# The opening of an FFT mixer with a two-layer network behind it: stage A on four array quarters, bias over 128 rows, turning by products over row halves

## The chip, the core and the metric

One core of a Trainium2 chip runs the kernel. The metric is the device time of one execution in microseconds (us), as the median of several runs. Engines: PE multiplies matrices (its weight loads are shown as PEld), DVE and ACT work on elements, SP issues most transfers, ACT a few; 16 DMA engines carry them.

## What is computed

x has 8 batches of 3008 x 256 numbers, in float32.

```python
X = np.fft.rfft(x, axis=1)
Yr = Xr @ w_r - Xi @ w_i + b_r
Yi = Xr @ w_i + Xi @ w_r + b_i
Yr = sign(Yr) * maximum(abs(Yr) - 0.01, 0)      # the same for Yi
y = np.fft.irfft(Yr + 1j * Yi, n=3008, axis=1)
h = maximum(y.reshape(24064, 256) @ w_in, 0)    # w_in: 256 x 2048
out = h * h @ w_out                             # w_out: 2048 x 256
```

## The kernel before

The transform of length 3008 is split as 47 x 64. Stage A multiplies x by a table over the 47 points; it gives 24 complex rows r, the others being conjugates. Stage B, for a pair of rows, transforms over the 64 points (`psb`), mixes by w_r and w_i (`psm`, with the bias as the first product of the sum), shrinks, and turns back over the 64 points (`psc`). Stage D goes back over the 47 points (`psd`) and leaves y in the chunk `xt`, split into a high and a low part. Between the stages the data go through DRAM: `s` holds the rows of A for B (`eva` stored, `bin` read back) and those of B for D (`evc` stored, `din` read back).

A long loop of rounds then runs the network: round r makes 256 of the 2048 hidden values for one chunk of about 508 tokens (`ph`, `mm1`) and, two rounds later, adds their share of the output (`po`, `mm2`). Stages A, B and D of the following batches are laid between its products. Batch 0 as a whole, stage A of batch 1 and the preparation of both weight matrices have to come earlier: that is the opening, the function `start()`.

`start()` does not issue instructions directly. It hands operations to a `Queue`: an engine (or a choice of two), a cost, a due date, the operations that must be over (`after`), those that must be issued (`behind`), and the buffer pool it takes from. `Queue.run()` simulates the engines with these costs and emits the instructions in the order that comes out; each engine then works through its own instructions strictly in that order. Dates and costs only set the order: on the chip every instruction waits for its data. The dates are lists of constants (`PAIR_DUE`, `A1_DUE`, `W_DUE`, `A2_DUE`); a load can be planned no earlier than its date unless the rings run empty.

Steps of the opening that the change touches, with their lines:

- Stage A of batch 0: x0 in nine loads (L454) over 96 partitions, which hold two points n2 times 47 rows (and two of filling). Sixteen products with the block table tU (96 x 96) over 512 columns each (L460), each copied by DVE (L472) and stored in two halves of 12 rows r: the first half on ACT's queue at once, the second on SP's queue (L476) once the loads of the first two pairs are issued.
- Stage A of batch 1: sixteen loads (L491, dates from `A1_DUE`), sixteen products (L460), copies (L498) into three `ev1` buffers, sixteen stores (L502).
- Twelve pairs: read-back (L524), `psb` (L320), high and low parts `xh`, `xl` (L533, L537), bias (L541: `one` is 33 x 128, `rows` 33 x 512; b's high part stands in row 0, its low part in row 32), eight products with the high part (L545), four with the low part (L550), `t` (ACT, L554), `z` (DVE, L558).
- Turning: two DVE copies (L564) and two ACT steps with a sign (L571) move the halves of z, 64 partitions each, under each other into `zh`; one product with tM (128 x 128) over 512 columns follows (L575), then the copy `evc` (L579).
- Weights: 16 blocks of 512 KB (L673, L675), each with a string of ACT and DVE steps (L684 to L746).
- The end: `din` for the first two groups of tokens (L619, L624), `psd` (L368), `dv` and `dx` (L632, L375), `xt` (L639, L642). Then the pools of the opening are given back and `ph` of round 0 can begin (L286 to L288).

Products of float32 operands show as two PE records each (the two of a 512-column product stand 0.43 us apart); those of the float32r type as one. In the loop, batches 2 to 7 have their stage A as four products of 47 x 64 against 512 columns, on the four quarters of the array (L845).

## Time and profile before

| | |
|---|---|
| median of 3 runs | 2592.77 us (2590.5 to 2596.39) |
| profiled execution | 2591.96 us, of which 2590.2 us from the first to the last instruction (the span) |
| PE, DVE, ACT busy | 99%, 81%, 77% of the span |
| mean granted PE clock | 0.996 |

Busy time of an engine counts only its computing instructions. A span of PE is longer than its step: records of consecutive products overlap, so the distance between two starts is the price of one. The granted clock is given as a share of 2.4 GHz; 0.50 is 1.2 GHz.

### The profile page before, as it was taken

How to read it: one execution, taken by the hardware profiler on the slowest of the kernel's cores; microseconds unless marked ns; L12 is line 12 of the kernel's file. 1: busy time of each engine (PE TensorE's matmuls, PEld its weight loads, DVE VectorE, ACT ScalarE, POOL GpSimd, SP SyncE). 2: the span in 40 equal slices, each digit the busy share in tenths (PEclk: the TensorE clock that was granted, in tenths of full speed). 3: DMA queues.
4: the chain of work that ended last, by engine and by line, in shares of the span. 5: the costliest groups of instructions: out<-in, count | busy, mean ns of one | idle time of the engine just before them, and what ended most of it. 6: DMA issues, size and time to landing. Idle time of an engine off the chain costs nothing.

```text
span 2590.2 us, 42989 instructions
## 1 busy us (share of the span) xinstructions
PE 2556.8 (99%) x16664; PEld 2273.7 (88%) x16664; DVE 2103.9 (81%) x3441; ACT 1990.5 (77%) x3048; POOL 0.2 (0%) x4
## 2 busy tenths in 40 slices
PE   7899999999999999999999999999999999999999
PEld 4589987999889998899988999899998999999998
DVE  6888887888878888788887888778887888877777
ACT  4687886788778787788877878778886788777776
POOL 0000000000000000000000000000000000000000
PEclk9999999999999999999999999999999999999999
DMA  8611114111241112311132111321114111001010
GB/s 251 219 52 41 42 51 142 48 44 50 66 124 32 49 41 84 105 40 41 47 113 79 36 41 50 124 61 36 57 41 129 49 46 56 32 25 35 17 32 17
DMA packets 125361, 171.35 MB, mean 66 GB/s; under 512 B 13157, under 2 KB 88751, under 8 KB 125159
## 3 DMA queue, kind: packets, MB, share of 16 engines
q1 hardware_dynamic: 124139, 166.99, 20.8%
q8 instruction: 133, 2.18, 0.3%
q10 hardware_dynamic: 1020, 1.61, 0.2%
q14 instruction: 69, 0.57, 0.1%
HBM read 93.50 MB, written 74.97 MB: 65 GB/s over the span
## 4 chain that ended last, share of the span: by engine, by line
PE 96%; DMA 2%; DVE 1%; ACT 1%; SPq 0%; issue 0%; ACTq 0%; DVEq 0%
PE ph L286 13%; PE ph L288 13%; PE ph L287 13%; PE po L286 12%; PE po L287 12%; PE po L288 12%; PE psd L368 3%; PE psb L320 3%; PE psm L288 2%; PE psm L287 2%; PE psm L286 2%; PE psa L845 2%; DMA s<-eva 1%; PE psm L545 1%; PE psa L460 1%; PE psc L287 1%
## 5 line engine op out<-in xcount | busy, mean ns | idle before, releaser
L1091 ACT CAST gh<-g 128x762 fp32r<-128x762 f32 (+3 forms) x768 | 682.4, 927 | 325.4 <-PE po L288 284.5
L1100 DVE TENSOR_TENSOR gl<-g,gh 128x762 fp32r<-128x762 f32 (+3 forms) x768 | 805.5, 1070 | 107.3 <-ACT gh L1091 106.4
L286 PE MATMUL po<-gh,wo 128*128 128x254 f32 (+1 forms) x2688 | 765.4, 285 | 0.0
L287 PE MATMUL po<-gl,wo 128*128 128x254 f32 (+1 forms) x2688 | 753.7, 280 | 0.4 <-DVE gl L1100 0.4
L288 PE MATMUL po<-gh,wo 128*128 128x254 f32 (+1 forms) x2688 | 753.0, 280 | 0.0
L286 PE MATMUL ph<-xt,wi 128*128 128x508 f32 (+2 forms) x1536 | 609.9, 397 | 8.9 <-ACT g L1038 5.2
L288 PE MATMUL ph<-xt,wi 128*128 128x508 f32 (+2 forms) x1536 | 598.4, 390 | 0.0
L287 PE MATMUL ph<-xt,wi 128*128 128x508 f32 (+2 forms) x1536 | 597.3, 389 | 0.0
L286 PEld LDWEIGHTS po<-gh,wo 128*128 128x128 f32 x2688 | 510.0, 190 | 35.9 <-issue 29.2
L1038 ACT ACTIVATE g<-ph 128x508 f32<-128x508 f32 (+1 forms) x768 | 410.9, 588 | 157.3 <-PE ph L288 154.5
L287 PEld LDWEIGHTS po<-gl,wo 128*128 128x128 f32 x2688 | 509.8, 190 | 6.8 <-DVE gl L1100 0.6
L288 PEld LDWEIGHTS po<-gh,wo 128*128 128x128 f32 x2688 | 509.8, 190 | 0.0
L1047 DVE TENSOR_TENSOR g<-g 128x508 f32<-128x508 f32 (+1 forms) x384 | 261.3, 680 | 279.3 <-ACT g L1039 272.7
L1039 ACT ACTIVATE g<-g 128x1016 f32<-128x1016 f32 (+1 forms) x384 | 401.3, 1045 | 12.2
L286 PEld LDWEIGHTS ph<-xt,wi 128*128 128x128 f32 x1536 | 290.1, 189 | 65.3 <-issue 9.7
L288 PEld LDWEIGHTS ph<-xt,wi 128*128 128x128 f32 x1536 | 289.4, 188 | 62.3
L287 PEld LDWEIGHTS ph<-xt,wi 128*128 128x128 f32 x1536 | 290.1, 189 | 45.3
L1048 DVE TENSOR_TENSOR g<-g 128x254 f32<-128x254 f32 (+1 forms) x384 | 161.6, 421 | 13.2
L1049 DVE TENSOR_TENSOR g<-g 128x254 f32<-128x254 f32 (+1 forms) x384 | 161.5, 421 | 13.2
L288 PE MATMUL psm<-wm,xl 128*128 128x256 f32 x504 | 140.3, 278 | 0.4 <-DVE xl L889 0.4
L287 PE MATMUL psm<-wm,xh 128*128 128x256 f32 x504 | 140.3, 278 | 0.0
L286 PE MATMUL psm<-wm,xh 128*128 128x256 f32 x504 | 140.2, 278 | 0.0
(104 smaller groups left out, 2449.6 us busy)
## 6 DMA issues: line engine op xcount, KB each, us to landing
bin<-s SPq DMA_DIRECT2D x96, 256.0 KB
s<-evc SPq DMA_DIRECT2D x96, 256.0 KB
xin<-in_xp_dram SPq DMA_DIRECT2D x48, 512.0 KB
din<-s SPq DMA_DIRECT2D x94, 240.0 KB
s<-eva SPq DMA_DIRECT2D x208, 96.0 KB
outT_dram<-o SPq DMA_DIRECT2D x144, 127.0 KB
w<-in_moe_w_in_dram SPq DMA_DIRECT2D x8, 512.0 KB
w<-in_moe_w_out_dram SPq DMA_DIRECT2D x8, 512.0 KB
```

Of the source, the lines that this page charges most:

```text
L286: nc.tensor.matmul(out, l0, r0, start=start, stop=False, **kw)
L287: nc.tensor.matmul(out, l0, r1, start=False, stop=False, **kw)
L288: nc.tensor.matmul(out, l1, r0, start=False, stop=stop, **kw)
L320: nc.tensor.matmul(ps[:, k, :, q, :], tv[:, q, k], tB[:, 0:r + 2:r + 1], start=True, stop=True)
L368: nc.tensor.matmul(ps[:, k, part], t[:n, s:s + P], tD[:n, tab + part, :n], start=True, stop=True)
L1038: nc.scalar.activation(g[:, a:b + 1:b - a, :m], ph[:, :, t * t0:t * t0 + m], AF.Relu)
L1039: nc.scalar.activation(g[:, LATER - 1:, :m], g[:, LATER - 1:, :m], AF.Square)
L1047: nc.vector.tensor_sub(g[:, :2, :m], at[1][:, None].broadcast_to([P, 2, m]), ends)
L1048: nc.vector.tensor_sub(at[6], at[3], at[4])
L1049: nc.vector.tensor_sub(at[1], at[6], at[2])
L1091: nc.scalar.copy(gg[k][0][:, part, :m], hid[k][:, part, :m])
L1100: nc.vector.tensor_sub(gg[k][1][:, part, :m], hid[k][:, part, :m], gg[k][0][:, part, :m].bitcast(F32))
```

## The change

- x of batches 0 and 1 is laid out as 48 rows (47 and one of zeros) for each of two halves of the partitions, four points n2 in a row. Stage A is eight visits a batch; a visit is four products of 47 x 64 against 512 columns, one on each quarter of the array, into two PSUM banks, and two copies (ACT or DVE). tU, t_b0 and the loads of tQ and tB in the loop's rounds 10 and 40 go; tQ and tB are loaded in the opening.
- Rows of the first four pairs (16 of 48 part rows) are stored at once, half on SP's queue and half on ACT's; the other 32 after the loads of the first four pairs have been issued. Weights, tB's rest, the signs and tC come behind these four loads too.
- Batch 1: two loads of 192 KB a visit into three buffers, not planned before their date; four `ev1` buffers, four stores of 96 KB a visit.
- Bias: `one` and `rows` have 128 rows, zeros but for two.
- Turning: one ACT step gives half of z its signs in place; four products follow, each over 64 rows (one half of the partitions) and 256 columns, two adding up in each of two banks. One such pair of banks is kept for them; the pool for all else has 6 banks for 8.
- Six products of 48 rows x 512 columns, whose result is not used, go to PE after stage A of batch 0 and ahead of the first pair; four of 512 columns after the last turning, ahead of `psd`.
- New due dates; the queue prefers an operation whose date lies 10 earlier when it is ready in time; weights and `wo` tiles follow the new layout.

```diff
-BUFS = dict(bin=4, evc=3, ev1=3, xh=2, xl=2, t=1, z=2, zh=2, x1=8, w64=4, w32=2, w7=2)
-HURRY = 20.0
-A2_DUE = [32 + i for i in range(N2 // 4)]
-PAIR_DUE = [24 + 5.0 * i for i in range(NPAIR)]
-A1_DUE = [60 + 3.4 * i for i in range(N2 // 4)]
-W_DUE = [30 + 4.6 * i for i in range(2 * NU)]
+BUFS = dict(bin=4, evc=3, ev1=4, xh=2, xl=2, t=1, z=3, x1=3, w64=4, w32=2, w7=2)
+FIRST_R = 8
+WARM = 6
+HURRY = 10.0
+A2_DUE = [24 + i for i in range(N2 // 8)]
+PAIR_DUE = [22 + 5.2 * i for i in range(NPAIR)]
+A1_DUE = [72 + 5.0 * i for i in range(N2 // 8)]
+W_DUE = [22 + 4.6 * i for i in range(2 * NU)]
...
+                urgent = [x for x in ops if x[1] < due - self.URGENT and x[0] < t + o.cost]
+                t, due, _, o = min(urgent, key=lambda x: x[:3]) if urgent else (t, due, _, o)
...
+    def rows_b(dma, scr, i, t):
+        v = scr.rearrange("(r c) (n d) -> (c n) r d", c=2, d=D)
+        dma(out=t.rearrange("p (q d) -> p q d", q=2), in_=v[:, 2 * i:2 * i + 2, :])
+
+    def rows_a(dma, scr, n, e, lo, hi):
+        dma(out=scr[:, n * D:(n + 2) * D], in_=e[lo:hi])
...
+    def points_a(o, t):
+        for c in range(2):
+            for h in range(2):
+                rows = slice(64 * h, 64 * h + N1)
+                nc.tensor.matmul(o[h][64 * c:64 * c + 64], tQ[rows], t[rows, 2 * D * c:2 * D * (c + 1)], start=True, stop=True)
...
-            ones = tl("z", bufs=2, name="ones")[:33]
-            one = tMs[:33, 0, :]
-            nq = N2 // 4
+            zero = tl("z", bufs=BUFS["z"], name="zero")
+            one = tMs[:, 0, :]
...
+            sg_in = load(36, 28, lambda: dma(out=sg, in_=sgn), behind=first_pairs)
+            tc_in = load(128, 28, lambda: dma(out=tC, in_=t_c), behind=first_pairs)
...
-                nc.tensor.matmul(o, tU, t, start=True, stop=True)
...
+                for g0, g1 in (((0, 1), (1, 2), (2, 4)), ((0, 2), (2, 4)))[k]:
+                    for h in range(2):
+                        n = load(192 * (g1 - g0), 0.1 + 0.01 * len(x0_in), lambda t=t, k=k, g0=g0, g1=g1, h=h: dma(
+                            out=t[64 * h:64 * h + ROWS, g0:g1, :],
+                            in_=xu[0, h].rearrange("p (g m) -> p g m", g=nv)[:, nv // 2 * k + g0:nv // 2 * k + g1]))
+                        for g in range(g0, g1):
+                            x0_in.setdefault(nv // 2 * k + g, []).append(n)
...
+            def visit(due, t, after, frees, cost):
+
+                s = {}
+
+                def points():
+                    s["o"] = [pst("psa") for _ in range(2)]
+                    points_a(s["o"], t())
+
+                n = op("PE", cost, due, points, after=after, alloc="ps", frees=frees)
+                n.more.append(queue.Bank())
+                return s, (n, n.more[0])
...
+                            s["e"] = const.tile([P, 2, 2 * D], F32, tag=f"wo{v}", name=f"eva{v}")
+                        engine(e)(s["e"][:, h], s["o"][h])
+
+                    copied.append(op(("ACT", "DVE"), 0.65, 3 + 0.1 * v, out, after=[banks[0]], frees=[banks[h]]))
+
+                def keep(part, c, by, s=s, v=v):
+                    lo, hi = ((0, cut), (cut, 2 * NR))[part]
+                    to = scr1[0][part].rearrange("r (v h m) -> r v h m", v=nv, h=2)[:, v, :, 2 * D * c:2 * D * (c + 1)]
+                    by(out=to, in_=s["e"][64 * c + lo:64 * c + hi])
+
+                for c in range(2):
+                    by = ("SP", "ACT")[c]
+                    a_first.append(store(64, 5 + 0.1 * v, lambda keep=keep, c=c: keep(0, c, (dma, nc.scalar.dma_start)[c]),
+                                         0.45, by, after=copied))
+                    a_second.append(store(128, A2_DUE[v], lambda keep=keep, c=c: keep(1, c, dma), 0.45, after=copied,
+                                          behind=first_pairs))
...
+                x = [load(192, due - 9, lambda fetch=fetch: fetch(0), alloc="x1")]
+                x.append(load(192, due - 9, lambda fetch=fetch: fetch(1), behind=[x[0]]))
+                x[0].hold = True
+                s, banks = visit(due, lambda hold=hold: hold["t"], x, [x[0]], 1.2)
...
+                        rows_a(dma, scr1[1], 8 * v + 4 * h + 2 * c, s[h], 64 * c, 64 * c + 2 * NR)
+
+                    e = op(("ACT", "DVE"), 0.65, due + 1, out, after=[banks[0]], alloc="ev1", frees=[banks[h]])
+                    queue.release(e, [store(96, due + 5, lambda keep=keep, c=c: keep(c), 0.42, after=[e]) for c in range(2)])
...
+                part = int(2 * i >= FIRST_R)
...
+                    rows_b(dma, scr1[0][part], i - part * FIRST_R // 2, s["t"])
+
+                def warm(s=s):
+                    s["ps"] = pst("psb")
+                    for _ in range(WARM):
+                        nc.tensor.matmul(s["ps"], x0[1][:ROWS, 2, :P], x0[1][:ROWS, 3, :2 * D], start=True, stop=True)
...
+                def signs(s=s, i=i):
+                    nc.scalar.activation(s["z"][:, D:], s["z"][:, D:], AF.Copy, scale=sg[:, 2, i:i + 1])
 
                 def back(s=s):
-                    s["c"] = pst("psc")
-                    nc.tensor.matmul(s["c"], tM, s["zh"].rearrange("p q e -> p (q e)"), start=True, stop=True)
+                    s["c"] = pp.tile([P, 2, 512], F32, tag="c", name="psc", bufs=1)
+                    for c in range(2):
+                        for q in range(2):
+                            src = slice(64 * q, 64 * q + 64)
+                            nc.tensor.matmul(s["c"][:, q, :D], tC[src, c], s["z"][src, D * c:D * c + D], start=c == 0, stop=c == 1)
 
                 def out(e, s=s, i=i):
                     evc[i] = tl("evc", bufs=BUFS["evc"])
-                    engine(e)(evc[i], s["c"])
-
-                n = load(256, due - 5, fetch, after=(a_first, a_second)[half], alloc="bin")
-                if i < 2:
+                    engine(e)(evc[i].rearrange("p (q e) -> p q e", q=2), s["c"][:, :, :D])
+
+                n = load(256, due - 5, fetch, after=(a_first, a_second)[part], alloc="bin")
+                if i < 4:
                     first_pairs.append(n)
...
+                first = [op("PE", 0.86 * WARM, due, warm, after=a0_done, alloc="ps")] if i == 0 else []
+                b = op("PE", 1.0, due, points, after=[n, *first, *(tb_in if i >= 2 else tb_in[:1])],
+                       alloc=None if first else "ps", frees=[n])
...
-                v = op("DVE", 0.57, due + 7, turn_v, after=[z], alloc="zh")
-                a = op("ACT", 1.0, due + 7, turn_a, after=[v, sg_in])
-                queue.release(z, [v, a])
-                c = op("PE", 0.87, due + 9, back, after=[v, a, tm_in], alloc="ps", frees=[v])
-                e = op(("ACT", "DVE"), 0.6, due + 10, out, after=[c], alloc="evc", frees=[c])
+                a = op("ACT", 0.35, due + 7, signs, after=[z, sg_in])
+                c = op("PE", 1.05, due + 9, back, after=[a, tc_in], alloc="pc")
+                psc_last = [c]
+                queue.release(z, [c])
+                e = op(("ACT", "DVE"), 0.65, due + 10, out, after=[c], alloc="evc", frees=[c])
...
+                        nc.tensor.matmul(s["ps"], tC[:, 0], tB[:, :8].rearrange("p a m -> p (a m)"), start=True, stop=True)
...
+                w_ = op("PE", 3.5 if u == 0 else 0, end + 12 + u, warm if u == 0 else lambda s=s: s.update(ps=pst("psd")),
+                        after=[psc_last[0]], alloc="ps")
+                p = op("PE", 1.0, end + 12 + u, points, after=[w_, f, *f2, td_in], frees=[f])
...
-        at(10, "load", lambda: nc.sync.dma_start(out=tQ, in_=t_q))
-        at(40, "load", lambda: nc.sync.dma_start(out=tB, in_=t_b))
```

## Rows read from the trace of the kernel before

**Rows 1.** The page: the chain of work that ended last, by engine, in shares of the span.
```profile
PE 96%; DMA 2%; DVE 1%; ACT 1%; SPq 0%; issue 0%; ACTq 0%; DVEq 0%
```

**Rows 2.** Busy time by stretches. Columns: from and to, length, busy us (and instructions) of PE, PEld, DVE, ACT and POOL, then the granted clock, the DMA engines' share and GB/s.
```profile
0.00:10.00 10.00, 5.86 (x9) 2.16 (x10) 2.60 (x5) 2.11 (x3) 0.20 (x4) 1.00 0.77 205
...
4.00:10.00 6.00, 5.86 (x9) 2.16 (x10) 2.06 (x3) 0.00 (x0) 0.00 (x0) 1.00 1.00 258
...
58.00:105.00 47.00, 46.74 (x181) 29.40 (x181) 43.46 (x94) 37.26 (x69) 0.00 (x0) 1.00 0.88 277
...
0.00:120.00 120.00, 97.87 (x358) 59.89 (x359) 94.72 (x190) 69.52 (x129) 0.20 (x4) 0.93 0.79 245
...
1000.00:2590.00 1590.00, 1584.74 (x10508) 1426.81 (x10506) 1286.36 (x2080) 1230.23 (x1853) 0.00 (x0) 1.00 0.18 55
```

**Rows 3.** Instructions in order of time at the end of the opening. Columns: start, length, engine (SPq and ACTq are their queues' transfers), line, operation, output <- inputs, shape, count, and in brackets the idle time before with what ended it.
```profile
104.25 2.74 PE L460 MATMUL psa<-x,tU 96*96 96x512 f32 x6
...
104.45 0.69 DVE L579 COPY evc<-psc 128x512 f32<-128x512 f32 x1 [0.22 <-PE psc L575]
...
108.16 1.12 PE L368 MATMUL psd<-tD,din 120*128 120x120 f32 x8 [1.17 <-DVE eva L498]
...
110.27 0.46 SPq L491 DMA_DIRECT2D x<-in_xu_dram  x1
...
110.83 9.02 SPq L502 DMA_DIRECT2D s<-eva  x6
...
113.86 1.52 PE L460 MATMUL psa<-x,tU 96*96 96x512 f32 x2 [2.71 <-DMA x<-in_xu_dram]
...
114.46 1.20 DVE L642 TENSOR_TENSOR xt<-dx,xt 128x470 fp32r<-128x470 f32 x2
...
118.50 0.58 ACT L498 COPY eva<-psa 96x512 f32<-96x512 f32 x1 [2.21 <-DMA s<-eva]
...
119.14 0.76 PE L286 MATMUL ph<-xt,wi 128*128 128x470 f32 x1 [3.76 <-ACT eva L498]
...
119.47 0.29 DVE L738 TENSOR_TENSOR w<-w,w 128x128 f32<-128x128 f32 x1
...
125.34 0.99 ACT L1039 ACTIVATE g<-g 128x944 f32<-128x944 f32 x1
```

**Rows 4.** The same view at the front.
```profile
25.29 0.92 SPq L524 DMA_DIRECT2D bin<-s  x2
...
28.16 3.75 PE L320 MATMUL psb<-tB,bin 128*128 128x128 f32 x16 [7.89 <-DMA bin<-s]
...
31.84 0.75 PE L541 MATMUL psm<-rows,tMs 33*128 33x512 f32 x1
...
32.52 2.08 PE L545 MATMUL psm<-wm,xh 128*128 128x512 f32 x8
...
32.59 0.67 ACT L684 ACTIVATE w<-w 128x512 f32<-128x512 f32 x1
```

**Rows 5.** Stretches of 1 us, columns as in rows 2: the granted clock around PE's two pauses.
```profile
22.00:23.00 1.00, 0.00 (x0) 0.00 (x0) 0.00 (x0) 0.00 (x0) 0.00 (x0) 0.59 0.91 328
...
32.00:33.00 1.00, 1.00 (x3) 0.56 (x4) 0.43 (x1) 0.95 (x2) 0.00 (x0) 0.79 1.02 385
...
114.00:115.00 1.00, 1.00 (x2) 0.07 (x1) 1.00 (x2) 1.00 (x3) 0.00 (x0) 0.67 0.52 164
```

**Rows 6.** The chain that ended last, in order of time: start, length, what.
```profile
22.53 2.69 DMA s<-eva
...
64.01 0.42 PE psm L541
64.43 2.04 PE psm L545 x8
66.48 0.93 PE psm L550 x4
67.40 0.86 PE psc L575 x2
68.26 0.86 PE psa L460 x2
...
80.44 0.89 PE psb L320 x8
```

**Rows 7.** PE's instructions in order of time: from a psb to the bias, and a four-quarter visit of stage A in the loop, ahead of `po`.
```profile
56.62 1.05 PE L320 MATMUL psb<-tB,bin 128*128 128x128 f32 x8
...
57.60 0.49 PE L541 MATMUL psm<-rows,tMs 33*128 33x512 f32 x1
...
2016.12 1.09 PE L845 MATMUL psa<-xin,tQ 47*64 47x512 f32 x8
...
2017.14 0.38 PE L286 MATMUL po<-gh,wo 128*128 128x254 f32 x1
```

**Rows 8.** Groups of the first 125 us: line, engine, operation, names, shapes, count | busy us, mean ns of one | idle before.
```profile
L571 ACT ACTIVATE zh<-z,sg 64x256 f32<-64x256 f32 x24 | 12.2, 507 | 0.5
...
L564 DVE COPY zh<-z 64x256 f32<-64x256 f32 x24 | 6.9, 286 | 0.5
```

**Rows 9.** Issues of stores of `eva`: queue, count, ns of one issue (min/median/max), first and last start. L502 are the opening's for batch 1 (96 partitions), L308 the loop's (48 partitions).
```profile
L502 SPq DMA_DIRECT2D s<-eva x16: 737/752/982, 69.8 to 119.1; - x16
...
L308 SPq DMA_DIRECT2D s<-eva x192: 302/410/1895, 385.5 to 2019.3; - x192
```

More of the change, by code (lines that the diff above doesn't have):

```diff
@@ L237, in run @@
             if o.alloc:
[L238 removed]
+                used[o.alloc] += [o, *o.more]
             order.append((t, len(order), o, e))
@@ L679, in weight @@
                     return s, n, n
-                n = load(512, due - 6, fetch, alloc="w64", after=raw_used, behind=first_pairs)
+                n = load(512, 14.5 if early else due - 6, fetch, alloc="w64", behind=a_first[-4:] if early else first_pairs)
                 def magnitude():
```

215 lines of the change are left out of this document (87 added, 128 removed).

## The prediction

> **What bounds the kernel now.** I read the page's totals first, then the table of busy time by stretches, then the order of instructions at both ends of the opening, then its chain of waits and its groups.
>
> PE is 96% of the chain that ended last [rows 1]. The stretches show one long saturated part: from 1000 us on PE idles 5.3 us in 1590, while DMA is lightly used [rows 2]. The change touches only the opening and two table loads of the loop that nothing there waits for. So the time changes by as much as the first product of the loop (`ph`, at 119.14 us [rows 3]) moves, plus what its first rounds gain or lose.
>
> The opening has four parts. (a) To 28.16 us: x of batch 0 comes in, stage A runs as 32 matmul records of 16 products, its stores land, the first rows are read back [rows 4]. DMA moves 258 GB/s here at a share of 1.00 [rows 2]. (b) 28 to 32.4 us: the first products of stage B at half clock; the granted clock fell while PE had nothing to do for 7.89 us (it averages 0.59 from 22 to 23) and came back about 4.3 us after PE began again (0.79 from 32 to 33) [rows 4, 5]. (c) To 104.25: the twelve row pairs and stage A of batch 1. From 58 to 105 PE is busy 46.74 of 47 us, DVE 43.46, DMA a share of 0.88 [rows 2]: PE is the bound, with two others close behind. One pair costs PE 0.42 (bias) + 2.04 + 0.93 + 0.86 (`psc`) + 0.89 (`psb`) = 5.14, and one `psa` 0.86 [rows 6]. Twelve pairs and the 15 `psa` in this part are 61.7 + 12.9 = 74.6, with 2.2 for the slow clock 76.8, against 76.1 measured: nothing else is in it. (d) 104.25 to 119.14, 14.9 us in which PE mostly waits [rows 3].
>
> **The change, part by part.** *Front.* x is the same 3.1 MB, now 48 rows to each half of the partitions. PE's share falls (eight visits for sixteen products), so it is the transfers that count. Moved by 10 us: 2.05 MB [rows 2]. x, the table and the first-row stores of six visits (0.128 MB each) are about 3.97 MB, so the last x is there at 10 + 1.92 MB / 258 GB/s = 17.4. It feeds two visits. A visit is what the loop already runs: 2016.12 to 2017.14, or 1.02 us, and a gap of 0.09 ahead as at the bias [rows 7]; I take 1.12. Then 19.7; a copy 0.69 [rows 3], 20.4; issuing a store 0.41 [rows 9], landing 2.69 [rows 6], 23.5; the read-back took 28.16 - 25.29 = 2.87 [rows 4], so 26.4: **-1.8**. Bounds: x at 328 GB/s, as DMA manages from 22 to 23 [rows 5], 24.9; visits at half clock, 28.2. The change spreads these stores over two queues (ACT's 16 become 8), and SP, which now issues 8 of them between loads, also passes four read-backs ahead of the weights. That puts tB's rest, the weights and tC behind 1 MB, under 4 us at 258 GB/s; the first weight was used at 32.59 [rows 4], and DVE has the room shown below.
>
> *The six products ahead of the first pair* cost 6 x 0.86 = 5.2 at full clock, 19.7 to 24.9, inside the wait for the read-back that ends at 26.4. If PE is slow at first, as it was for 4.3 us after 28.16, that time does 2.5 of them and the rest takes 3.0: 7.3 us, so 27.0 to 28.8, and the front gains nothing. Either way the first pairs then run at full clock: sixteen `psb` records took 3.75 where two pairs cost 1.78, and the first bias 0.68 for 0.42 [rows 4, 6], so **-2.2** (bound 0, should the clock not rise).
>
> *Stage A of batch 1*: eight visits of 1.12 for the 15 products: 9.0 - 12.9 = **-3.9**. Its loads, held to dates, come in two halves; 16 copies stay 16, and its 32 stores of 0.41 issue cost SP 13.1 where 16 of 0.75 cost 12.0 [rows 9].
>
> *Bias*: 0.42 and a gap of 0.09 (the psb before it ends at 57.51, the bias starts at 57.60 [rows 7]) become a full-height product like its neighbours, 2.04 / 8 = 0.255: 0.26 a pair, **-3.1** (bound 0).
>
> *Turning.* Two DVE copies (6.9 us in all) go; two ACT steps of 0.507, over 64 partitions each, become one of the same length [rows 8], which saves ACT 6.1. PE's one product becomes four of half height and half length. No row has two row halves side by side with 128 columns. From below: as the quarters of `psa` do, two at a time, 0.86 and no more: 0. From above: four in turn, 4 x 0.43 + 0.26, +1.12 a pair, +13.4. I take 0.86 and the 0.26 that the visit of [rows 7] shows beyond a product of 0.86: **+3.1**; the visit is the same kind of split, so I stay near the low end. The single `psc` buffer makes one pair's products wait for the last pair's copy (0.69 at most [rows 3]), 5 us before: free. So does the pool of 6 for 8 banks; its cover is the copies' 0.7 us.
>
> Here one rule of the notes speaks against the change. The measured row says that a product of 33 rows takes 0.42 and one of 128 rows 0.255 [rows 6]. The Trainium skill, "TensorE: Matmul & The Clock Gate", section "Why this matters for your kernels", says that a single matmul with K=32 takes the same time as with K=128. By the row the bias gains 3.1 us; by the rule nothing, and the sum would be 3.1 higher, a rival below.
>
> *End.* After the last `psc` came 0.9 to its copy's end, 3.0 to the first `psd`, then `dv`, `dx` and `xt`, done at 115.66: 11.4 us. `ph` waited 3.5 more, for the last copy of batch 1's stage A, which itself waited for a buffer whose store was late, behind SP's 9.02 us of six stores [rows 3]. With eight visits on four buffers and half-size stores I let the 3.5 go and keep the 11.4: **-3.5** (bounds -5 and 0). The four products ahead of `psd` (3.4 us) fall in the 3.0 us in which the last rows travel; uncovered they cost 3.4. After `psd` PE idles some 4 us again (3.76 ahead of `ph` before, the clock falling at 114) [rows 3, 5]; I let `ph` run slow as before (bound -2.2, the front's price).
>
> **Sum**: -1.8 - 2.2 - 3.9 - 3.1 + 3.1 - 3.5 = -11.4, `ph` at 107.7. Covers: DVE. Its last weight step ended at 119.76 and its first use in the loop was 126.33, when L1039 ended, so it had 6.6 us to spare [rows 3]; with 6.9 less work it ends near 110 to 112 and is needed, at the same distance behind `ph`, at 114.9. DMA: 245 GB/s over 120 us are 29.4 MB [rows 2]; to move them by 107.7 takes 273 on average, and 259 without the 1.5 MB of batch 1's stores, which nobody awaits in the first rounds. The saturated stretch reached 277, the front 258 [rows 2]: that cover is thin. On the profiled execution's own 2591.96 (span 2590.2 and 1.76 around it) this is 2580.6; the median of the runs, 2592.77, lies 0.8 higher. I say **2581**.
>
> **Rivals.** *The end is set by batch 1's transfers.* Against the sum: its last load, dated 103 (111 - 8) in the code, was issued at 110.27 [rows 3], 7 us late; the new last date is 98, and the same lateness gives 105.3, its product 3.6 later as before (113.86), a visit at half clock 2.0 and two copies: `ph` near 112.5, 2585.4. If DMA only keeps its mean of 245 GB/s, 27.9 MB take 114 us: 2587, and all 29.4 take 120: no gain. For it: the thin cover. Against: PE, not DMA, was the bound while it ran at 277 [rows 2]. I give 2585 to 2591, centre 2587.5.
> *The bias gains nothing* (the rule above; as a mechanism, the 0.42 is the product's own time whatever its height): 2584. Against it is only that its neighbours of the same length take 0.255.
> *The halves of the turning run in turn*: the break-even lies at a `psc` of 0.86 + 11.4 / 12 + 0.26 = 2.07 a pair; four in turn reach 1.98, so 2591, and 2594 if the 0.26 comes twice a pair. Against: quarters in [rows 7].
> *Slower: 48-partition transfers run at half the rate.* The front needs 3.1 MB at 258 GB/s; at half it takes 12 us more, and the other 3.1 MB in part (c) want 12 us of an engine set that is 88% used, so up to 10 more: 2593 to 2603. It decides above a loss of 11 us, a rate under 135 GB/s. For it: no x load of before had 48 partitions. Against: two are always queued together, and the loop's stores of 48 partitions are issued in 0.41 where those of 96 took 0.75 [rows 9], so nothing there looks costlier.
>
> **How the numbers follow.** Chances: forecast 0.55 (its own range 2575 to 2587), bias 0.10, batch 1's transfers 0.20, halves in turn 0.06, slower 0.09. 0.2% is 5.2 us, about what a measurement of this kernel can tell from no change: below 2587.6 is faster, above 2598 slower. Faster: 0.55 + 0.10 + half of 0.20 = 0.75. Slower: most of 0.09, 0.07. Same: 0.18. The range 2574 to 2591 holds the first three; what lies above it is about 0.15.
>
> **What would show it.** Right: first `psb` near 26 with records 0.11 apart, bias 0.25, `psc` about 1.1 a pair, the last `psc` ending near 97, `ph` at 105 to 111, and the rounds after it as before. Wrong: x landing after 20 us; the six products ending after the read-back; `psc` at 1.7 or more; `ph` waiting for a copy, a store or a load of batch 1; or PE idle between pairs because DVE or DMA has become the bound in part (c).

## The result, and the profile after

The changed kernel takes 2609.64 us (median of 4 runs, 2608.44 to 2611.58) against 2593.0 before (2590.5 to 2596.39): a ratio of 1.0064 with a 95% interval of 1.0047 to 1.0081. It is slower by 0.6%, clear of the noise; 2581 was predicted. The profiled execution took 2608.44 with a span of 2606.6, so 16.5 us are to be found between the two traces. Taken at marks that both have:

| stretch | before | after | difference |
|---|---|---|---|
| start to first `psb` | 28.16 | 35.63 | +7.5 |
| first `psb` to end of the last `psc` | 76.3 | 78.0 | +1.7 |
| last `psc` to first `ph` | 14.7 | 16.1 | +1.4 |
| first `ph` to first `po` | 14.2 | 14.5 | +0.3 |
| first `po` to the 377th of 382 groups of `po` (below: the loop) | 2417.2 | 2422.4 | +5.2 |
| rest | 39.6 | 40.0 | +0.4 |

The front, PE in order of time (columns as in [rows 3]); it answers [rows 4]:

```profile
16.53 4.01 PE L324 MATMUL psa<-x,tQ 47*64 47x512 f32 x16 [0.29 <-DMA x<-in_xu_dram]
21.49 3.68 PE L324 MATMUL psa<-x,tQ 47*64 47x512 f32 x14 [0.94 <-DMA x<-in_xu_dram]
25.10 10.60 PE L551 MATMUL psb<-x 48*128 48x512 f32 x12
35.63 3.78 PE L332 MATMUL psb<-tB,bin 128*128 128x128 f32 x16
```

Two visits (16 records) take 4 us, where the loop's visit of [rows 7] takes 1.02. Twelve records of the six products take 10.6 us, 0.85 each, which is half speed (1.2 GHz; 0.43 is full). The sixteen `psb` records behind them still take 3.78, as in [rows 4]. And the last x lands at 21.4. The read-back is later still, as SP's queue shows:

```profile
28.83 0.36 SPq L501 DMA_DIRECT2D s<-eva  x1
...
30.83 1.93 SPq L304 DMA_DIRECT2D bin<-s  x4
```

The last copy of stage A ended at 25.89, but its store stood behind three loads and two other stores in SP's order. The granted clock has no entry in the trace before 39.6 us, so the stretches print 1.00 there; the lengths of the records tell the speed. By stretches (columns as in [rows 2], which these answer):

```profile
4.00:10.00 6.00, 5.01 (x17) 1.44 (x18) 1.38 (x2) 1.17 (x2) 0.00 (x0) 1.00 1.06 192
10.00:20.00 10.00, 9.39 (x34) 2.23 (x33) 2.08 (x3) 1.76 (x3) 0.00 (x0) 1.00 0.99 187
...
58.00:105.00 47.00, 45.63 (x254) 33.35 (x253) 42.38 (x83) 32.93 (x64) 0.00 (x0) 1.00 0.86 258
```

192 GB/s at a DMA share of 1.06, where [rows 2] has 258 at 1.00: the engines are as busy and move less. Next the middle, PE:

```profile
47.38 0.70 PE L596 MATMUL psc<-z,tC 64*128 64x256 f32 x4 [1.77 <-DVE z L586]
48.56 0.70 PE L596 MATMUL psc<-z,tC 64*128 64x256 f32 x4 [0.47 <-ACT z L589]
50.80 2.08 PE L596 MATMUL psc<-z,tC 64*128 64x256 f32 x8 [1.54 <-ACT wi L746]
52.81 3.78 PE L332 MATMUL psb<-tB,bin 128*128 128x128 f32 x16
```

and ACT beside it:

```profile
40.29 0.68 ACT L714 ACTIVATE w<-w 128x512 f32<-128x512 f32 x1 [0.26 <-DMA w<-in_moe_w_in_dram]
...
45.55 0.68 ACT L714 ACTIVATE w<-w 128x512 f32<-128x512 f32 x1 [1.17 <-DMA w<-in_moe_w_in_dram]
46.76 0.62 ACT L746 CAST wi<-w 128x512 fp32r<-128x512 f32 x1 [0.53 <-DVE w L730]
47.42 0.69 ACT L582 ACTIVATE t<-psm,neg 128x512 f32<-128x512 f32 x1
```

The step `t` of the second pair (L582) stands behind two weight steps that waited for a weight and for DVE. PE idles, its clock falls again, and the second pair's `psc` and two `psb` run at half speed. The end, PE:

```profile
112.50 1.14 PE L596 MATMUL psc<-z,tC 64*128 64x256 f32 x8
113.56 3.70 PE L653 MATMUL psd<-tB,tC 128*128 128x512 f32 x8
119.23 2.02 PE L380 MATMUL psd<-tD,din 120*128 120x120 f32 x16 [1.97 <-DMA din<-evc]
121.17 1.95 PE L324 MATMUL psa<-x,tQ 47*64 47x512 f32 x16
125.98 2.55 PE L324 MATMUL psa<-x,tQ 47*64 47x512 f32 x8 [2.86 <-DMA x<-in_xu_dram]
129.73 0.76 PE L287 MATMUL ph<-xt,wi 128*128 128x470 f32 x1 [1.20 <-ACT eva L527]
```

and SP's queue:

```profile
120.52 1.84 SPq L307 DMA_DIRECT2D s<-eva  x4
122.46 0.85 SPq L518 DMA_DIRECT2D x<-in_xu_dram  x2
```

`ph` waits for the copy of batch 1's last visit, whose x was issued at 122.46, behind stores. Its date in the code is 98.

### The profile page after: what moved, and what is told of

Its sections match the earlier page's. It is cut to its first block, busy times and chain, and to the rows that moved or that the text cites. A ratio compares the mean times of both kernels' runs of the same rounds, so it can differ in the third digit from the quotient of the medians.

```text
span 2606.6 us, 43276 instructions
## 1 busy us (share of the span) xinstructions
PE 2577.2 (99%) x16820; PEld 2282.1 (88%) x16820; DVE 2092.9 (80%) x3411; ACT 1987.8 (76%) x3042; POOL 0.2 (0%) x4
## 4 chain that ended last, share of the span: by engine, by line
PE 95%; DMA 2%; DVE 1%; ACT 1%; issue 0%; SPq 0%; ACTq 0%; DVEq 0%
PE ph L287 13%; PE ph L288 13%; PE ph L289 13%; PE po L287 12%; PE po L288 12%; PE po L289 12%; PE psd L380 3%; PE psb L332 3%; PE psa L324 2%; PE psm L289 2%; PE psm L288 2%; PE psm L287 2%; PE psc L287 1%; PE psc L288 1%; PE psc L289 1%; PE psm L573 1%
```

## The experiments

All times are medians of the device time; the kernel before, measured beside each, took 2592.9 to 2593.5. Where one run is all there is, no ratio is given. "Loop" is as in the table above.

| run | time us | ratio to before (95%) | first `psb` | last `psc` ends | `ph` | loop |
|---|---|---|---|---|---|---|
| no six products | 2608.68 | 1.0062 (1.0047 to 1.0077) | 34.85 | 114.4 | 129.8 | 2423.3 |
| six over 128 rows | 2608.48 | 1.0058 (1.0041 to 1.0075) | 34.28 | 112.7 | 129.4 | 2423.4 |
| weights due at 30 | 2603.02 | 1.0038 (1.0023 to 1.0053) | 36.45 | 112.1 | 130.4 | 2417.0 |
| x on two queues | 2611.89 | 1.0071 (1.0056 to 1.0086) | 38.61 | 117.4 | 133.7 | 2422.5 |
| bias 33 rows | 2613.11 (one run) | | 36.60 | 116.8 | 133.7 | 2422.5 |
| xt first | 2603.79 | 1.0045 (1.0028 to 1.0061) | 35.54 | 112.6 | 129.5 | 2417.9 |
| batch 1 early | 2599.99 | 1.0026 (1.0015 to 1.0037) | 34.60 | 115.5 | 126.1 | 2416.3 |
| one visit a load | 2606.82 (one run) | | 33.83 | 112.1 | 127.7 | 2422.5 |
| before, x by 48 rows | 2592.2 (one run) | | 30.23 | 105.8 | 119.8 | 2417.0 |
| before, x at 0 and 64 | 2602.56 (one run) | | 37.21 | 115.7 | 130.2 | 2416.8 |
| x over 128 rows | 2604.05 (one run) | | 29.74 | 107.2 | 124.1 | 2423.8 |
| old stage A | 2591.81 | 0.9997 (0.9988 to 1.0006) | 29.81 | 105.6 | 119.8 | 2417.0 |
| old stage A, dates | 2592.06 | 0.9998 (0.999 to 1.0007) | 28.98 | 102.8 | 118.5 | 2418.2 |
| same, weights spread | 2597.74 | 1.0018 (1.0008 to 1.0028) | 29.70 | 102.4 | 114.4 | 2417.1 |
| same, visits earlier | 2596.27 | 1.0011 (1.0002 to 1.002) | 29.77 | 104.8 | 117.3 | 2415.8 |
| before, bias 128 rows | 2590.01 | 0.9991 (0.9982 to 1.0) | 28.72 | 102.0 | 116.9 | 2417.8 |
| all put right | 2597.73 | 1.0015 (1.0006 to 1.0023) | 27.23 | 109.5 | 123.5 | 2417.1 |
| same, batch 1 whole | 2598.02 | 1.0018 (1.0009 to 1.0027) | 27.56 | 110.2 | 124.5 | 2418.5 |

### The six products

Taken away (`for _ in range(WARM)` becomes `range(0)`):

> Changed kernel without the six products ahead of the first pair; every engine's order is otherwise the same. Theory A (at 48 rows the six products ran at half clock, 0.85 us a record, and did not bring the clock up, so they only delay): the first psb starts when its read-back lands, 30.8 + 2.9 (before: issued 25.29, psb 28.16) = 33.7 us instead of 35.63; psb x16 still takes 3.8 us and full speed still comes about 3.8 us after the first psb; the order behind it is the same, so ph starts some 2 us earlier, at 127 to 129, and the time is 2606 to 2609. Rival B (the products do keep the clock from falling lower or shorten the wait for full speed): psb x16 longer than 4.2 us or the first mix at half speed (L573 x8 over 3 us), and ph no earlier than 129.5, time 2609 to 2612.

```profile
34.85 3.75 PE L332 MATMUL psb<-tB,bin 128*128 128x128 f32 x16 [8.64 <-DMA bin<-s]
```

The pair starts 0.8 us earlier and waits for its read-back; `ph` stays where it was. A's mechanism holds, and so does its size: x came 1.0 us later in this run (the last two visits start at 22.52, 21.49 above), and from there to the first `psb` are 12.3 us instead of 14.1. The six products cost 1.8 us (2 expected) and gave nothing.

```
- matmul(s["ps"], x0[1][:ROWS, 2, :P], x0[1][:ROWS, 3, :2 * D], ...)
+ matmul(s["ps"], made[5]["e"][:, 0, :P], made[5]["e"][:, 1], ...)
```

> Changed kernel with the same six products taken over 128 rows by 128 columns (from the stage A copy of the sixth visit) in place of 48 rows; their result is discarded as before and the order is the same. Theory A (what was missing is height: products of 48 and 47 rows run at half clock however many there are, products of 128 rows bring the clock up some 4 us after they begin, as psb did at 28.16 in the kernel before): the twelve records begin at 25.1 and take 4 us at 0.85 and the rest at 0.43 each, 7 us in all instead of 10.6; the first psb starts at 33 to 34 (its read-back) and x16 takes 1.9 to 2.1 us if the clock holds through the wait; first mix 4 us earlier; ph at 125.5 to 128; time 2604 to 2608. Rival B (height is not it): 10.6 us again and psb x16 3.8 us, ph 129 to 130, time 2608 to 2612.

```profile
25.54 6.47 PE L554 MATMUL psb<-eva 128*128 128x512 f32 x12
34.28 3.52 PE L332 MATMUL psb<-tB,bin 128*128 128x128 f32 x16 [2.26 <-DMA bin<-s]
```

Of twelve records over 128 rows, two took 1.01 and 0.85, one 0.58 and the rest 0.43: the clock rose under them, where it had not in 10.6 us of 48-row records. Then PE idled 2.26 us and the `psb` ran at half speed again (granted 0.50 from 35 to 37). So A is right on what brought the clock up, and the gain was lost in a pause. Without the pause it would have met the next wait: the first `psc` starts at 47.24, after 3.29 us of waiting for `z`, and at 47.38 in the changed kernel. The run of the kernel before with 48-row products (below) says the same of the clock from the other side.

### What the first batch's x waits for

```
- n = load(..., lambda ...: dma(                          # both halves by SP
+ n = load(..., by=("SP", "ACT")[h], do=lambda ...: (dma, nc.scalar.dma_start)[h](
```

> Changed kernel with the x loads of the upper row halves issued by ScalarE and those of the lower by SyncE, so that packets of both halves are under way at once; sizes and counts stay. Theory A (a transfer into 48 partitions is slow because all packets under way at a time go to one band of partitions: 8 KB packets 749 ns against 256 ns for 4 KB over 96 rows in the kernel before): 8 KB packets fall to 550 ns or less, 4 to 20 us moves 240 GB/s or more instead of 190, last x lands before 18.5 (21.5), first psb at 31 to 33 (it waits for the six products), ph 126 to 128, time 2605 to 2608. Rival B (each engine's rate for rows this long is what it is): packets within 10% of 749 ns, last x after 20.5, ph 129 to 130.5, time 2608 to 2612.

200 and 206 GB/s in the two first stretches (192 and 187), 8 KB packets at 599 to 718 ns on the mean, by queue and stretch: somewhat faster than 749, but short of what A asks. The first `psb` came 3 us later; that ACT's copies and issues now compete is a guess. The run decides for neither theory.

```
- for g0, g1 in (((0, 1), (1, 2), (2, 4)), ((0, 2), (2, 4)))[k]:
+ for g0, g1 in ((0, 1), (1, 2), (2, 3), (3, 4)):
```

> Changed kernel whose first batch is loaded one visit and one row half at a time: sixteen transfers with rows of 4 KB instead of four with 4 KB and six with 8 KB. Theory A (what is slow is the long row: 8 KB packets took 749 ns where two of 4 KB take 590): packets of 4 KB at 300 ns or less, 205 GB/s or more over 4 to 20 us instead of 190, last x lands 1.5 to 3 us before 21.5. Rival B (the engines are slow because all rows of a transfer go into 48 partitions; the length does not matter): 4 KB packets at 340 ns or more, last x at 21 or later.

191 and 194 GB/s, 4 KB packets at 354 and 286 ns on the mean of the two stretches: the length of the row is not it. The first `psb` came 1.8 us earlier all the same.

```
- out=t[:NU1, g0:g1, :], in_=xu[0, :, ...]                          # before: 96 rows
+ out=t[48 * h:48 * h + 48, g0:g1, :], in_=xu[0, 48 * h:48 * h + 48, ...]  # h = 0, 1
```

> Kernel before, with one thing changed: each transfer of the first batch's x (96 partitions) is issued as two of 48 partitions, the rows of each partition as long as before. Theory A (a transfer into 48 partitions moves fewer bytes a microsecond: 258 GB/s over 4 to 10 us became 192 in the changed kernel): 4 to 20 us moves 185 to 210 GB/s, 4 KB packets take 285 ns or more (254), stage A ends 3 to 5 us later than 20.3, first psb at 31 to 33.5 (28.16), time 2595 to 2599. Rival B (the lower rate of the changed kernel comes of something else, such as its second queue's stores of few rows): 245 GB/s or more, first psb before 29, time within 2 us of 2593.

```profile
4.00:10.00 6.00, 6.00 (x8) 1.87 (x9) 2.06 (x3) 0.00 (x0) 0.00 (x0) 1.00 0.90 253
```

B on the rate: 253 GB/s, near the 258 of [rows 2]. So 48 partitions alone don't give the 192. The first `psb`, at 30.23, is still 2 us later than before and later than B allows. Then the same two halves at partitions 0 and 64, as the changed kernel has them (`out=t[64 * h:64 * h + 48, ...]`; the product takes `x0[..][:48]` alone, so half of stage A is left out):

> Kernel before with the first batch's x in two transfers of 48 partitions each, into partitions 0 to 47 and 64 to 111 (0 to 47 and 48 to 95 in the run before this, which still moved 253 GB/s over 4 to 10 us). Batch 0's stage A multiplies the lower 48 rows alone, so half of it is left out; only the transfers are looked at. Theory A (rows 0 to 47 and 64 to 111 together are what the engines are slow on, as the changed kernel uses them): 205 GB/s or less over 4 to 10 us, 4 KB packets at 285 ns or more. Rival B (the place is not it): 240 GB/s or more, 4 KB packets at 260 ns or less; then what remains is the array that is read or the number of transfers in flight.

```profile
4.00:10.00 6.00, 6.00 (x8) 1.88 (x7) 2.06 (x3) 0.00 (x0) 0.00 (x0) 1.00 0.76 202
```

```profile
3.50 27.59 PE L470 MATMUL psa<-x,tU 48*96 48x512 f32 x32 [3.50 <-DMA x<-in_xu_dram]
```

202 GB/s from 4 to 10 as A has it, but a share of only 0.76 and packets of 246 ns as B has it, 231 from 10 to 20: undecided. What it does show is the clock. Thirty-two records over 48 rows took 27.6 us, with starts 0.85 apart throughout; over 96 rows, before, they took 16.12, with starts 0.43 apart from the seventh on.

Last, x padded to 64 rows a half, so that one transfer fills 128 partitions:

```
- out=t[64 * h:64 * h + ROWS, g0:g1, :], in_=xu[0, h]...    # for h in range(2)
+ out=t[:, g0:g1, :], in_=xz...[:, ...]                     # one transfer, a third more bytes
```

> Changed kernel with batch 0's x padded to 64 rows a half in the input, so that each transfer fills all 128 partitions: five transfers of 512 KB to 1 MB instead of ten, a third more bytes (4.2 MB instead of 3.1). Theory A (place or short height slows the transfers): 255 GB/s or more over 4 to 20 us, last x at 18 to 19.5 instead of 21.5 although it moves more. Rival B (the rate stays at 190): last x at 25 or later, first psb at 29 or later with the six products ahead of it, ph 3 us later than 129.7.

```profile
4.00:10.00 6.00, 4.93 (x24) 1.36 (x28) 1.38 (x2) 1.17 (x2) 0.00 (x0) 1.00 1.04 429
```

429 GB/s where the changed kernel has 192, at much the same share (1.04 and 1.06); 8 KB packets took 310 ns instead of 749. A holds. Stage A then ends at 19.3 and the first `psb` starts at 29.74, 5.9 us earlier, right behind the six products, which now are in its way. `ph` is 5.7 us earlier. That the transfers' shape (two halves of 48 rows in ten transfers, where this run has five over all partitions) costs the front some 6 us is shown. What in the halves is slow stays open: with halves at 0 and 48 the rate was as before, and the run at 0 and 64 was undecided.

### Weights, dates, and where x lies

`W_DUE = [30 + 4.6 * i ...]` in place of 22:

> Changed kernel with the due times of the weight steps put back from 22 to 30 us (the spacing stays at 4.6). Theory A (TensorE's idle stretch from 45.4 to 50.8 and the half-clock psc and psb behind it come from weight steps that stand ahead of the first pairs' shrink and signs on VectorE and ScalarE, and that wait for weights landing at 40 us): idle time between 36 and 60 us falls from 4 to 5 us to under 2.5, no half-clock psb at 52.8 (x16 3.78 us), last psc 5 to 9 us earlier (103 to 108 instead of 112.5), ph at 122 to 126, time 2601 to 2606. Rival B (the end is set by batch 1's transfers and the last loads on SP's queue, whatever the pairs do): last psc earlier, yet ph within 2 us of 129.7, time 2607 to 2611.

```profile
48.98 1.13 PE L596 MATMUL psc<-z,tC 64*128 64x256 f32 x8 [0.69 <-ACT evc L600]
50.04 2.05 PE L332 MATMUL psb<-tB,bin 128*128 128x128 f32 x16
54.29 2.12 PE L573 MATMUL psm<-wm,xh 128*128 128x512 f32 x8 [1.96 <-ACT xh L561]
```

The second half-speed stretch is gone, as A says, but the idle time is not: new waits of 2 us appear at 54 and 65, where a pair's split comes late. The first of these splits stood on ACT behind a weight step (L746) that had waited 3.64 us for DVE. In all PE idles 5.4 us between the first `psb` and the last `psc`, 5.1 in the changed kernel. `ph` came no earlier: B was right on `ph`. What the time fell came from the loop, 2417.0 instead of 2422.4, which neither theory had. The instructions of the loop are the same in both. What differs is where the two `xt` tiles of the first chunk lie: of the tiles that share four buffers, the first to be written gets the first places. To test it, ACT writes two columns of each `xt` at the start:

```
+ for x in xt:
+     nc.scalar.copy(x[:, 0, :2], zero[:, :2])
```

> Changed kernel in which two small ScalarE copies into the two xt tiles stand at the very start, so that xt is the first to be written of the tiles that share those four buffers; the first x of the loop then lies at bytes 40768 and 48896 of each partition (8128 apart, as in the kernel before: 40672 and 48800) instead of 44832 and 48896 (4064 apart). The opening is otherwise the same, and the copies are idle-time work of 0.1 us. Theory A (the loop's extra 5.2 us, from the first output product to the last 2422.4 us against 2417.2, comes of where the two x tiles lie): 2417 plus or minus 1 here, ph at 129 to 130.5, time 2602 to 2606. Rival B (it comes of the opening's new order or of the chip's state): 2422 plus or minus 1, time 2608 to 2612.

A: the loop takes 2417.9, the time falls by 5.9 and `ph` stays at 129.5. In the thirteen profiles with the two tiles 8128 bytes apart the loop took 2415.8 to 2418.5, before among them; in the seven with 4064 bytes between them (which leaves the two places 12192 apart for the next chunk) 2422.4 to 2423.8. The cost grows evenly over the rounds. In the groups of products from 400 to 2300 us, changed kernel first, then this run (count | busy us, mean ns of one):

```profile
L287 PE MATMUL ph<-xt,wi 128*128 128x506 f32 x196 | 78.6, 401 | 0.0
...
L288 PE MATMUL psm<-wm,xh 128*128 128x256 f32 x432 | 120.8, 280 | 0.0
```

```profile
L287 PE MATMUL ph<-xt,wi 128*128 128x506 f32 x200 | 79.5, 397 | 0.0
...
L288 PE MATMUL psm<-wm,xh 128*128 128x256 f32 x432 | 120.0, 278 | 0.0
```

Some products that read the tiles (those over 506 columns), and some beside them that don't, take 1 to 4 ns less; those over 508 columns stay within 1 ns, those over 470 take up to 2 ns more. What in the chip makes the distance count is open.

`A1_DUE = [60 + 5.0 * i ...]` in place of 72:

> Changed kernel with the due times of batch 1's eight visits 12 us earlier (60 to 95 instead of 72 to 107). It happens to place the xt tiles at 44832 and 52960, 8128 apart. Theory A (ph waits for the last visit because its x is issued only at 122.46, behind stores on SyncE): the last x is issued by 113, the last visit ends before the unfolding of the first groups, ph follows the unfolded tiles at 124 to 126.5; with the xt tiles 8128 apart the loop takes 2417, time 2597 to 2601 (2602 to 2606 if the place of the tiles is not what costs 5 us). Rival B (visits put earlier push the pairs later by as much, since TensorE is full from 70 us on): last psc at 117 or later, ph at 128.5 or later, time above 2602.

```profile
119.02 1.09 PE L324 MATMUL psa<-x,tQ 47*64 47x512 f32 x8
121.67 2.02 PE L380 MATMUL psd<-tD,din 120*128 120x120 f32 x16 [1.56 <-DMA din<-evc]
126.13 0.48 PE L287 MATMUL ph<-xt,wi 128*128 128x470 f32 x1 [2.44 <-ACT eva L527]
```

The last x is issued at 108.33; `ph` starts 3.6 us earlier, within A's range as the time is, though the last `psc` ends 1.8 later. So A holds, and B has a small part: the pairs do come later.

### The bias alone

`one[:33], rows[:33]` in the changed kernel:

> Changed kernel with the bias product back on the first 33 of the same 128 rows; nothing else. Theory A (the prediction's step: 0.42 at 33 rows belongs to a change of the tile between a short and a full-height product, and full height saves 0.25 of it): from the bias to the first product of the mix 0.42 here against 0.23 (behind the mix's own products) and 0.34 (behind turning, unfolding or visits) in the changed kernel, 1 to 2.5 us over 12 pairs of TensorE's time, ph up to 2 us later. Rival B (the rows don't matter; what 0.42 to 0.43 holds is mostly the turn from full-precision products to those at four times the rate): 0.34 and 0.23 here too, ph within 0.7 of 129.7.

```profile
84.47 0.58 PE L569 MATMUL psm<-rows,tMs 33*128 33x512 f32 x1
84.97 2.12 PE L573 MATMUL psm<-wm,xh 128*128 128x512 f32 x8
86.94 1.10 PE L578 MATMUL psm<-wm,xl 128*128 128x512 f32 x4
```

The changed kernel, behind the same turning:

```profile
81.93 0.50 PE L569 MATMUL psm<-rows,tMs 128*128 128x512 f32 x1
82.27 2.03 PE L573 MATMUL psm<-wm,xh 128*128 128x512 f32 x8
84.13 1.10 PE L578 MATMUL psm<-wm,xl 128*128 128x512 f32 x4
```

From 84.47 to 86.94 the bias and the eight products behind it take 2.47; over 128 rows, from 81.93 to 84.13, 2.20. Behind a `psb` it is 2.39 (80.27 to 82.66) against 2.17 (77.68 to 79.85). So full height saves 0.22 to 0.27 a pair, and about half of it lies in the products behind the bias: A. That is 2.6 to 3.2 us over twelve pairs; `ph` came 3.9 later in this single run, more than A allows, so part of that has another cause (the first `psb` was already 1.0 later). The same edit on the kernel before, and nothing else (`rows` and `one` over all 128 partitions):

> Kernel before with the bias product over all 128 rows, the other rows zero, and nothing else changed. Theory A (as the 33-row run of the changed kernel showed, where the bias and the eight products behind it took 2.40 us against 2.19: a short product makes itself and the products behind it longer): bias to the end of the eight products 2.2 instead of 2.45, TensorE's time 0.2 to 0.25 us less a pair, last psc 1.5 to 3 us earlier than 104.25, time 1 to 3 us less than before. Rival B (VectorE, busy 9.0 to 9.4 of every 10 us there, sets the pairs' rate, and TensorE only waits longer): the same shorter products, yet last psc within 0.7 us and time within 1 us of before.

```profile
63.70 0.47 PE L541 MATMUL psm<-rows,tMs 128*128 128x512 f32 x1
64.01 2.00 PE L545 MATMUL psm<-wm,xh 128*128 128x512 f32 x8
65.85 1.08 PE L550 MATMUL psm<-wm,xl 128*128 128x512 f32 x4
```

0.31 + 1.84 where [rows 6] has 0.42 + 2.04. First `psb` to last `psc` takes 73.3 instead of 76.3, and `ph` starts at 116.85. That is A. The time, 2590.01, lies 2.9 us under the kernel before, at the edge of what can be measured (0.9982 to 1.0). It is the only version whose whole interval lies at or under the kernel before.

### The old stage A with the rest of the change, and everything put right

Batch 0's stage A as before, the rest as changed. In this run and the next, batch 1's stage B reads the table in batch 0's row order: the load of the table in batch 1's order is left out, so batch 1 is computed from the wrong rows, with the same work and, but for that load, the same transfers.

> Changed kernel with batch 0's stage A put back as it was before (x over 96 partitions, one 96-row product a visit, its two row halves of twelve first-points stored and read back as before, the first tB table with its rows in the old order, no six products); batch 1, the bias, the turning and every due time of the pairs and weights as changed. The xt tiles come to lie 8128 bytes apart, as before. Theory A (the front is the largest loss, and it is carried to the end): first psb at 28 to 29 us, full speed 4 us later (39.4 in the changed kernel), ph at 121 to 125 instead of 129.7, loop 2417 from first to last output product, time 2594 to 2599. Rival B (the front's loss is taken up by waits further on, for weights and for batch 1's x, so that undoing it gains little): ph after 126.5, time 2601 or more.

`ph` at 119.8, time 2591.8: undoing one part takes back 10 us of `ph` and, with the tiles 8128 apart here, the whole loss, more than A expected. What stays of the change is then worth nothing against before. With the dates as well (`W_DUE` at 30, `A1_DUE` at 60, `xt` first):

> As the kernel with the old stage A of batch 0, and also: due times of the weight steps back at 30, batch 1's visits due at 60 to 95 instead of 72 to 107, and xt written first so that its two tiles lie 8128 bytes apart. What stays of the change: batch 1 on quarters, the bias over 128 rows, the turning by products. Theory A (these three are worth what the rows say, about 5 us of TensorE's time for batch 1 and 2.5 for the bias against 2.5 lost in turning, once the front, the order behind late weights and the late x are out of the way): no idle stretch over 1.5 us between 36 and 100 us, last psc at 101 to 105, ph at 114 to 119, time 2586 to 2593, faster than before. Rival B (what stands after the last psc, the last groups' round trip and the last visit, is longer than before and takes the gain back): ph at 120 or later, time 2594 or more.

```profile
106.39 1.09 PE L339 MATMUL psa<-x,tQ 47*64 47x512 f32 x8
112.79 3.74 PE L395 MATMUL psd<-tD,din 120*128 120x120 f32 x16 [5.31 <-DMA din<-evc]
118.47 0.76 PE L302 MATMUL ph<-xt,wi 128*128 128x470 f32 x1 [1.94 <-ACT xt L694]
```

The last `psc` ends 1.6 us earlier than before, the last visit 8, and the last groups' read-back comes so late that `ph` gains 0.7. All lies within A's ranges, but the time is the kernel before's (0.999 to 1.0007), not faster. Two attempts to get it out earlier, by later weight steps:

> The old stage A for batch 0 with the changed kernel's batch 1, bias and turning, as two runs ago, with the weight steps due at 30 and 5.6 us apart instead of 4.6, batch 1's visits due at 60 to 92, xt written first, and the table of stage B reloaded in batch 1's row order before batch 1 needs it (the earlier two runs read batch 1 through batch 0's table). Theory A (there SyncE stood 6.9 us at stores that waited for copies behind weight steps, so the last groups' read-back was issued at 105.4 and psd started at 112.8, 10 us after the last psc; weight steps due later let the copies through): read-back issued by 101, psd at 105 to 108, ph at 111 to 115, time 2584 to 2589. Rival B (VectorE and ScalarE are full, so the steps that are put later hold the end up elsewhere): ph at 117 or later, time 2590 or more.

> As the run before it with the weight steps 5.2 us apart and batch 1's visits due at 56 to 88, so that the last visit stands ahead of the last psc. Same theories: A, ph at 111 to 115 and 2584 to 2589; B, ph at 117 or later and 2590 or more.

```profile
114.41 0.48 PE L302 MATMUL ph<-xt,wi 128*128 128x470 f32 x1 [2.06 <-ACT xt L694]
...
128.81 0.76 PE L302 MATMUL ph<-xt,wi 128*128 128x470 f32 x1 [9.54 <-ACT g L1091]
```

In the first `ph` started 4.7 us earlier than before, and PE then stood 9.5 us in the first rounds, while ACT and DVE were still at the weights. The gain was given back one stage later: B named the full engines, but not that `ph` would come early. In the second `ph` started at 117.3 and the time is B's.

Last, the changed kernel with all of it: x over 128 rows, eight products over 128 rows, the dates, `xt` first; then batch 1's x whole too.

> Changed kernel with what the runs put right, all together: batch 0's x in whole 128-partition transfers (429 GB/s over 4 to 10 us in the run of them alone), eight products over 128 rows in place of six over 48 (6.5 us for six where those took 10.6; eight reach to the read-back, so that no pause of 2 us lets the clock fall again), weight steps due at 30, batch 1's visits due at 60 to 95, xt written first. Theory A (front, clock, order and place of the tiles are the whole loss, and stage A on quarters is then worth its sum): visits end at 19 to 19.5, first psb at 27 to 28.5 with x16 in 2.0 to 2.4, last psc at 100 to 104, ph at 112 to 117, loop 2417, time 2583 to 2590, faster than before. Rival B (what follows the last psc, or VectorE with the weights, takes the gain): last psc at 105 or later or ph at 118.5 or later, time 2592 or more.

> As the run before it, and batch 1's x too in whole 128-partition transfers (eight of 512 KB instead of sixteen of 192 KB, two buffers instead of three), six buffers instead of four for its copies, and its stores due 9 us after the visit instead of 5, so that SyncE stands less at stores that wait for copies. Theory A (SyncE's issues are what is late at the end): last groups' read-back issued by 102, psd within 5 us of the last psc, ph 2 to 4 us earlier than in the run before it. Rival B (the copies and weight steps on ScalarE and VectorE are late themselves, whoever issues): ph within 1 us of the run before it.

```profile
19.37 8.02 PE L555 MATMUL psb<-eva 128*128 128x512 f32 x16
27.23 1.95 PE L332 MATMUL psb<-tB,bin 128*128 128x128 f32 x16
...
41.77 3.62 PE L332 MATMUL psb<-tB,bin 128*128 128x128 f32 x16 [2.85 <-DMA tB<-in_t_b_dram]
...
56.34 2.08 PE L600 MATMUL psc<-z,tC 64*128 64x256 f32 x8 [3.87 <-DVE z L590]
```

The front does what the change meant: first pair at 27.23 (26.4 was forecast) and at full speed, 8.4 us earlier than in the changed kernel. Then PE waits for the rest of tB, for `z` behind weights, and falls to half speed twice; the last `psc` ends at 109.5, only 4 us earlier. Rival B, for both.

## Why the prediction was wrong, point by point

*Front, -1.8: wrong by 9 us.* Its step "1.92 MB / 258 GB/s, last x at 17.4" took a rate of 96-partition transfers for other ones. Measured: 187 to 192 GB/s, the last x used at 21.49: 4.1 us. The second step, "a visit is what the loop already runs, 1.02", was right only at full clock: visits took 2, which is 1.4 us more for the last two. That bound stood in the prediction (28.2); it was not joined with the late x. Two more steps were short: the last first-row store was to be issued as soon as its copy ended and went out 2.9 us later on SP's queue, so the read-back was issued 1.8 us later than summed; and the six products, outside the wait after all, held the pair up by another 1.9. The rival "48-partition transfers" named the front, but asked for half the rate, where a quarter less was enough, and the run of the kernel before with such transfers at 0 and 48 shows that 48 partitions are not the reason by themselves.

*Six products and clock, -2.2: wrong.* Either branch assumed that they bring the clock up, and only the bound of 0 allowed for what came. Products of 47 and 48 rows ran at half speed from the first visit to 35.6 us; under products of 128 rows, in the run above, full speed came with the fourth record. The gain was 0, and a second half-speed stretch at 50.8 cost about 3 (`psc` 2.08 for 1.04, two `psb` 3.78 for 1.95).

*The cover of DVE: wrong.* I checked DVE's sum of work and not its order. The weights' first date went from 30 to 22, the pairs' only from 24 to 22, the front came late, and the first weight landed at 40: the shrink (`t` and `z`) and `signs` of the first pairs stood behind weight steps on ACT and DVE. DVE's last weight step ended at 126.2, where 110 to 112 was forecast. PE idled 5.1 us between first `psb` and last `psc`, 1.7 before. The dates alone don't explain it, since with the weights due at 30 PE idled 5.4.

*Bias, -3.1: right, in part by luck.* The kernel before with that edit alone takes 3.0 us less in part (c). Half of the saving or more lies in the products behind the bias, so the reason given (a product's own 0.42 against 0.255) was at most half of it: the bias itself still takes 0.31 to 0.34. (The end of `psb` at 57.51, from which the gap of 0.09 comes, is its start and a price of 0.89; its row in [rows 7] runs to 57.67.) The rival by the Trainium skill, "TensorE: Matmul & The Clock Gate", section "Why this matters for your kernels" (K=32 takes the time of K=128), doesn't hold for this place: 33 rows cost 0.2 to 0.3 us more than 128, with the products behind them.

*Stage A of batch 1, -3.9: right in the price* (1.02 to 1.09 a visit, 1.12 taken), though the count was not: 12 or 13 of the 16 products stood ahead of the last `psc` before, not 15, so the sum that met 76.1 had no room for the 1.7 us of idle time; and of the eight visits five stood ahead of it after. *Turning, +3.1: right*, 1.06 a pair for 0.86, +2.4.

*End, -3.5: wrong by 5.* The rival "batch 1's transfers set the end" was what happened: its last x was issued 24 us after its date, not 7. SP had 33 other transfers to issue in that time (15.4 us), and waited the rest, longest 2.5 us ahead of a store of `evc`.

*Not in the prediction at all:* the loop's 5.2 us. "The loop is not touched" was true of its instructions, not of its tiles.

The miss by stretches: front 9.3, middle 7.8, end 4.9, first rounds 0.3, loop 5.2, rest 0.4, together 27.9 where 27.8 us lie between 2608.44 and 2580.6. The middle is put down to the clock (2.2 not gained and 3 more) and to idle time (3.4), less 0.7 for the cheaper turning; that this comes to 7.9 is in part luck, as three of the visits counted there fell behind the last `psc`. Yet once they were put right one by one, the sum still did not come out: each gain on PE ran into the work of ACT and DVE or SP's queue. DVE had stood close behind PE already, busy 43.46 of 47 us [rows 2].

## What to carry to other kernels

A rate, a clock or a price read from a trace belongs to the shape it was read at: before summing, ask whether the new transfer fills as many partitions and the new product as many rows. Where a queue is ordered by dates, changing one list of dates changes who waits for whom on every engine, and a sum of busy time doesn't see it. And when a loop that was not edited gets slower, compare where its tiles lie.

## What was not expected of the hardware

- Transfers into 128 partitions moved 429 GB/s from 4 to 10 us; the changed kernel's, in halves of 48 rows at partitions 0 and 64, moved 192, at much the same DMA share.
- The clock did not rise under 32 records over 48 rows, which stayed 0.85 apart for 27.6 us; records over 128 rows were 0.43 apart from the fourth on.
- A bias product over 33 rows lengthens the eight full-height products behind it by 0.11 to 0.2 us.
- Two operand tiles 4064 bytes apart instead of 8128 made the same loop 0.2% slower.
